# Sink scores turned by VectorE and gathered by DMAs instead of turned by TensorE, with unread products in TensorE's planned waits

## The chip, the core and the metric

The kernel runs on one NeuronCore of one Trainium2 chip. The core has a matrix engine (TensorE, "PE" in the profile, with its weight loads as "PEld"), three engines for elementwise work (VectorE "DVE", ScalarE "ACT", GpSimd "POOL") and SyncE ("SP"), which here issues every DMA. Each engine runs its own instructions in order and waits on semaphores for the others. [...] The metric is the time of one execution in microseconds on the device.

## What is computed

Attention with a causal window of 128 and a few "sink" keys at the front that every query may see, then a two-layer network with a squared ReLU:

```python
scores = scale * np.matmul(q, k.transpose(0, 1, 3, 2))       # 4 batches, 8 heads, 768 positions, 64 wide
keep = is_sink | in_window                                   # 4 sinks, window 128
scores = np.where(keep, scores, -1000000000.0)
a = np.exp(scores - max); a = a / (a.sum + 1e-09)
x = np.matmul(a, v)                                          # as 3072 tokens x 512
h = np.maximum(x @ w_in, 0.0)                                # w_in 512 x 2048
out = h * h @ w_out                                          # w_out 2048 x 512
```

The weights arrive as float64, read as pairs of 32-bit words; q, k and v are fp32.

## The kernel before

The work is cut into 8 chunks of 384 tokens (`TOK`; half a batch each, so that even chunks are first halves) and each chunk's attention into 4 pairs of heads: 32 pairs `s`. For accuracy most products run in parts: a number is split into a rounded fp32r part and the rest, and high x high, high x low and low x high are added in PSUM.

**A pair's attention** (`attention`). SP loads q, k and v (L410, L405, L417). TensorE makes scores of 3 blocks of 128 queries for two heads (`score`, L483 in plain fp32 for the first 8 pairs, called `plain`, L489 with split operands for the others). A block of scores has up to 264 columns (`BAND`): 128 keys of the block before, 8 sink columns (`NS`), 128 of its own. DVE masks it, takes the maximum and brings it to SBUF as `P` (L466), ACT takes the exponential (L472), DVE forms the reciprocals (L529, L530), and POOL scales (L537), or ACT for some blocks of the early pairs (L535).

The scaled scores must be turned before the product with v. For the first 8 pairs (`turned`) TensorE turns blocks of 128x128 (L638) and ACT or DVE copies them out of PSUM (L600). For the other 24, DVE turns 32x32 blocks (L668, L672) into `T`, SP sends `T` by four DMAs to a DRAM buffer `via` (L685) and fetches it in the right order by a fifth into `PT` (L698).

**The sinks** go another way. POOL copies the sink columns twice as a high part (L552) and once as the rest (L550) into `PSK`, 128 queries by 128 columns of which three groups of 32 hold something. TensorE turns each block of `PSK` (`turn_sinks`, L590: three blocks a pair, two in a first half, which skips its first block for `i0` = 1), and ACT or, for the 24 later pairs, DVE copies the result from PSUM into `SK` (L600).

`values` forms the output: products of `PT` (or the turned blocks) with v, both heads side by side in plain fp32 (L726), and one product of `SK` with `VS`, the values at the sinks (L730; `sinks` loads them and splits them at L368, L374 and L379). ACT and DVE split the result into `xh` and `xl` (L742, L747).

**The network** (`products`). For each of 16 slices `fc` of the hidden layer 12 products of 384 columns (L778) go into one bank, ACT and DVE form the square and its rest (L791, L795, L800, L807), and 9 products of 512 columns (L823) add to three output banks. Outputs leave through L864 and L877. The legs are chunk 0 with the first half of the slices, chunk 1 with all, chunk 0 with the rest, then chunks 2 to 7. The attention of the next chunk is spread between the products of the present one.

**The weights** come in 32 rows (`row_steps`): three DVE operations on integers (L303, L310, L317), a rounding copy on ACT (L323), and the rest on DVE or POOL (L327). A check of the weights (`check_steps`) loads halves of rows again (L339) for ACT (L344, L351).

**The order** is worked out before the program is written. `add` records steps with an engine, an expected cost, a rank (a due time, smaller is earlier), the cells they read and write, and the PSUM banks they take from a pool or give back. `Plan.order` then walks through time: for each engine it collects the steps that could start, takes the earliest (among those within 0.03 us the lowest rank), and emits it. A step may list several engines, with a handicap for some (`LOW_DVE`, `SC_ACT`, `CP_DVE`). A DVE step marked `"port"` and a POOL step are planned not to overlap. A change of TensorE's mode is planned at 0.17 us. DMAs are planned `LATE` = 1 us later than their cost says. What the plan emits stands in each engine's queue in that order; the real waits are semaphores between them.

## Time and profile before

| what | value |
|---|---|
| median of 3 runs | 690.72 us (690.72 to 690.74) |
| profiled execution | 688.96 us |
| its span, first to last instruction | 686.9 us |
| PE busy | 667.4 us, 97%, 3722 instructions |
| DVE busy | 459.1 us, 67% |
| ACT busy | 375.0 us, 55% |
| POOL busy | 215.2 us, 31% |
| DMA | 104.78 MB, mean 153 GB/s |
| mean granted TensorE clock | 0.991 |

The profiled execution was shorter than the median of the runs by 1.76 us, and 2.06 us of it lie outside the span. Matmuls are pipelined, so the length of one overlaps the next, and what a group of them costs is read from the start of one group to the start of the next. A "wait" is idle time of an engine with the instruction that ended it. The chain of waits follows the end of the program back from step to step. Stretches of the span show which engine is full at what time: the start, with little network work, is quite unlike the rest.

### The profile page before, as it was taken

Reading aid. Unit: us, or ns where it says so; the run is one execution under the profiler, and the core shown is the slowest. Engines: PE = TensorE matmul, PEld = TensorE weight load, DVE = VectorE, ACT = ScalarE, POOL = GpSimd, SP = SyncE. Lnnn points to the kernel's source line nnn. Section 1 sums busy time; section 2 is a strip of 40 time slices with the busy share of each in tenths; the row PEclk is TensorE's granted clock in tenths of the full one; section 3 lists DMA queues with packets and bytes.
Section 4 is the critical chain, followed back from the end, with each engine's and each line's share of the span. In section 5 each row is a group of like instructions: output and inputs, shape, how many; then the busy total and the mean of one; then the engine's idle time right before and its main releaser. Section 6 shows DMA issues by size and latency. Waiting matters only on the chain.

```text
span 686.9 us, 11380 instructions
## 1 busy us (share of the span) xinstructions
PE 667.4 (97%) x3722; PEld 581.1 (85%) x3722; DVE 459.1 (67%) x1194; ACT 375.0 (55%) x1073; POOL 215.2 (31%) x377
## 2 busy tenths in 40 slices
PE   4999989999999999999999999999999999999996
PEld 3667879998888888888888898888898888899985
DVE  7599999967987655676677766666776764242222
ACT  6798734355464434456666656666666565442221
POOL 4455433534544513232244323223332322000000
PEclk9799999999999999999999999999999999999999
DMA  7746455215777532466556666555557754310001
GB/s 244 220 163 203 168 192 183 84 52 157 223 245 227 154 106 93 134 207 193 155 148 184 211 188 201 170 167 174 145 169 213 223 160 114 116 51 12 0 1 51
DMA packets 58178, 104.78 MB, mean 153 GB/s; under 512 B 6208, under 2 KB 34624, under 8 KB 58112
## 3 DMA queue, kind: packets, MB, share of 16 engines
q1 hardware_dynamic: 58112, 103.98, 49.7%
q8 instruction: 31, 0.51, 0.3%
q14 instruction: 35, 0.29, 0.1%
HBM read 79.58 MB, written 24.38 MB: 151 GB/s over the span
## 4 chain that ended last, share of the span: by engine, by line
PE 90%; DVE 6%; ACT 1%; issue 1%; DMA 1%; SPq 0%; POOL 0%; DVEq 0%
PE bank L823 37%; PE bank L778 37%; PE bank L726 6%; PE bank L489 5%; PE bank L730 1%; DVE f L310 1%; PE bank L590 1%; PE bank L483 1%; DVE P L466 1%; PE bank L638 1%; DVE f L317 1%; DVE f L303 1%; DMA kn<-in_k_dram 1%; ACT w L323 0%; DVE w L327 0%
## 5 line engine op out<-in xcount | busy, mean ns | idle before, releaser
L778 PE MATMUL bank<-x,w 128*128 128x384 f32 x1536 | 303.1, 339 | 0.7 <-DVE gl L807 0.7
L778 PEld LDWEIGHTS bank<-x,w 128*128 128x128 f32 x1536 | 267.0, 188 | 9.5 <-issue 1.4
L823 PE MATMUL bank<-w,gh 128*128 128x512 f32 x768 | 242.7, 397 | 2.1 <-ACT ob L864 2.1
L823 PEld LDWEIGHTS bank<-w,gh 128*128 128x128 f32 x768 | 137.5, 188 | 21.4 <-ACT ob L864 2.4
L823 PE MATMUL bank<-w,gl 128*128 128x512 f32 x384 | 151.4, 394 | 0.0
L446 POOL TENSOR_TENSOR KS<-kn,KS 128x408 fp32r<-128x408 f32 (+1 forms) x48 | 64.9, 1352 | 225.1 <-DVE KS L441 164.2
L791 ACT ACTIVATE r<-bank 128x384 f32<-128x384 f32 x128 | 62.7, 490 | 129.3 <-PE bank L778 128.2
L472 ACT ACTIVATE P<-P,nbs 128x264 f32<-128x264 f32 (+1 forms) x192 | 94.4, 492 | 66.5 <-DVE nbs L466 65.7
L800 DVE TENSOR_TENSOR bank<-bank,r 128x384 f32<-128x384 f32 x128 | 72.1, 563 | 83.4 <-ACT r L791 83.1
L537 POOL TENSOR_SCALAR P<-P,small 128x128 f32<-128x128 f32 (+1 forms) x168 | 88.5, 543 | 71.1 <-DVE small L530 48.9
L823 PEld LDWEIGHTS bank<-w,gl 128*128 128x128 f32 x384 | 72.1, 188 | 16.6
L466 DVE CUSTOM_DVE_ANT_0 P<-bank,maskA 128x264 f32<-128x264 f32 x128 | 53.4, 426 | 45.1 <-PE bank L489 43.6
L807 DVE TENSOR_TENSOR gl<-bank,gh 128x384 fp32r<-128x384 f32 x128 | 70.9, 554 | 17.4 <-ACT gh L795 11.8
L795 ACT ACTIVATE gh<-r 128x384 fp32r<-128x384 f32 x128 | 66.7, 521 | 4.7 <-PE bank L823 2.2
L668 DVE STREAM_TRANSPOSE T<-P 128x384 f32<-128x384 f32 x96 | 45.2, 495 | 22.6 <-POOL P L537 21.7
L489 PEld LDWEIGHTS bank<-KS,QS 128*128 128x128 f32 x288 | 51.6, 188 | 6.2 <-DVE nbs L466 0.4
L489 PE MATMUL bank<-KS,QS 128*128 128x264 f32 (+1 forms) x288 | 55.4, 279 | 0.0
L742 ACT CAST x<-bank 128x384 fp32r<-128x384 f32 x32 | 15.3, 478 | 52.6 <-PE bank L730 52.4
L327 POOL TENSOR_TENSOR w<-f,w 128x512 fp32r<-128x512 f32 x19 | 27.1, 1430 | 51.4 <-ACT w L323 51.4
L726 PE MATMUL bank<-PT,vn 128*64 128x256 f32 (+1 forms) x392 | 40.6, 347 | 0.0
L726 PEld LDWEIGHTS bank<-PT,vn 128*64 128x64 f32 x392 | 25.7, 139 | 15.5 <-issue 6.7
L529 DVE TENSOR_TENSOR small<-small,eps 128x3 f32<-128x3 f32 (+1 forms) x56 | 34.5, 616 | 3.3 <-ACT P L472 2.7
(90 smaller groups left out, 575.5 us busy)
## 6 DMA issues: line engine op xcount, KB each, us to landing
raw<-in_moe_w_dram SPq DMA_DIRECT2D x32, 512.0 KB, 3.7
half<-in_moe_w_dram SPq DMA_DIRECT2D x64, 256.0 KB, 3.6
via<-T SPq DMA_DIRECT2D x48, 192.0 KB, 3.7
PT<-via SPq DMA_DIRECT2D x12, 768.0 KB, 4.4
via<-T SPq DMA_DIRECT2D x48, 160.0 KB, 4.2
PT<-via SPq DMA_DIRECT2D x12, 640.0 KB, 4.7
kn<-in_k_dram SPq DMA_DIRECT2D x24, 272.0 KB, 4.4
qn<-in_q_dram SPq DMA_DIRECT2D x32, 192.0 KB, 3.6
```

The source lines that it names most:

```text
L446: lambda h=h: nc.gpsimd.tensor_tensor(KS(h)[:, 1, 0:nk], kn()[:, h, 0:nk], f32(KS(h)[:, 0, 0:nk]), op=ALU.subtract),
L466: nc.vector.tensor_tensor_reduce(Pt(h)[:, i, o : o + n], ps_[:, 0:n], mask[:, 0:n], -SCALE, BIG, ALU.add, ALU.min, nb)
L472: nc.scalar.activation(Pt(h)[:, i, o : o + n], Pt(h)[:, i, o : o + n], AF.Exp, bias=nb, scale=-1.0, accum_out=sm[:, h, i : i + 1],)
L489: nc.tensor.matmul(bank(key)[:, 0:n], QS(h)[:, cols], flat[:, a, c0 : c0 + n], start=(a == 0), stop=(a == 1),)
L537: {"POOL": nc.gpsimd, "DVE": nc.vector}[engine].tensor_scalar(a, a, rs[:, h, i : i + 1], 1.0, op0=ALU.mult, op1=ALU.mult)
L726: nc.tensor.matmul(xo[h * D : h * D + D, qs[0] * P : qs[0] * P + len(qs) * P], vn[:, kk, h, :], rhs(), start=(n == 0), stop=False, skip_gr ...
L778: nc.tensor.matmul(bank(key)[:, 0:TOK], wi[fc][:, i, cc * P : (cc + 1) * P], xt[:, cc, :], start=(cc == 0 and j == 0), stop=(cc == NCC - 1 ...
L791: lambda key=key, r=r: nc.scalar.activation(r(), bank(key)[:, 0:TOK], AF.Relu),
L795: ("ACT", 0.41), n - 9, lambda gh=gh, r=r: nc.scalar.activation(gh(), r(), AF.Square),
L800: lambda key=key, r=r: nc.vector.tensor_tensor(bank(key)[:, 0:TOK], bank(key)[:, 0:TOK], r(), op=ALU.mult),
L807: lambda key=key, gh=gh, gl=gl: nc.vector.tensor_tensor(gl(), bank(key)[:, 0:TOK], f32(gh()), op=ALU.subtract),
L823: nc.tensor.matmul(bank(okey), gt()[:, ts_], wo[f][:, i, :], start=(f == f0 and j == 0), stop=(f == f1 - 1 and j == 2),)
```

## The change

`NS` goes from 8 to 4, which is the number of sinks in the inputs (more of them, found at run time, send the program to its general path). So a block of scores has at most 260 columns, the k blocks are 132 wide instead of 136, and the three parts of two heads' sinks fit in 24 columns.

For the 24 later pairs TensorE no longer turns the sinks. POOL writes the parts into a `PSK` of 32 columns a block, DVE turns it in 32x32 blocks into `SKT`, four DMAs bring the four groups of 32 queries onto the same 32 partitions (in `VR`, which the loads of the sink values share), and ACT or DVE copies that into `SK`, rounded. `SK` is now laid out by group of 32 queries, block, query, and the sink product reads it in runs of 32. For the first 8 pairs TensorE still turns, from a wider `PSK`.

The plan's rules change: POOL and DVE are planned to hold each other up for half a step only (`SHARE`); a step within 0.15 us that is due more than 8 earlier goes first (`HOLD`); TensorE is planned to start at 6.5 us; the early pairs' scaling may go to DVE too (`SC_DVE`); the later pairs' scores are planned to wait for their buffer `P` (`CLAIM`); the mode change costs 0.2, and the values product counts as another mode at its start.

Where TensorE is planned to wait more than 0.4 us for a step that takes a bank, before 24 us of planned time, `fill` puts products of `ident` with itself into that bank, for half of the wait at 0.22 us each. Nobody reads them. As the planned start is 6.5 us, there are none ahead of the first score.

```diff
-NS = 8
+NS = 4
...
+SHARE = 0.5
+HOLD = 0.15
+SC_DVE = 0.3
+CLAIM = (True, False)
+WARM = 24.0
+FULL = 0.5
...
-        free = dict(PE=0.0, DVE=5.5, ACT=1.5, POOL=5.0, SP=0.5)
+        free = dict(PE=6.5, DVE=5.5, ACT=1.5, POOL=5.0, SP=0.5)
...
                 a = min((a for a in able if a[0] <= first + 0.03), key=lambda a: a[1:3])
+                urgent = [x for x in able if x[0] <= first + HOLD and x[1] < a[1] - 8]
+                if urgent:
+                    a = min(urgent, key=lambda a: a[1:3])
...
             if e == "PE":
-                cost += 0.17 * (kind[0] != mode)
-                mode = kind[0]
+                if picks and WARM > t > free[e] + 0.4:
+                    yield lambda i=picks[0], n=int((t - free[e] - 0.2) * FULL / 0.22): self.fill(i, n)
+                cost += 0.2 * (kind[0] != mode)
+                mode = kind[-1]
             free[e] = t + cost
...
-                    port[e] = t + cost
+                    port[e] = t + SHARE * cost
...
         VS = wp.tile([P, NPAIR, P], F32R, name="VS")
-        PSK = [sb("PSK", [P, NQ, P], F32R, "PSK_0"), sb("w23", [P, NQ, P], F32R, "PSK_1")]
-        for t in (VS, *PSK):
+        PSK = [wp.tile([P, NQ, 32], F32R, name=f"PSK{i}") for i in range(2)]
+        SKT = wp.tile([P, NQ, 32], F32, name="SKT")
+        SK = [sb("SK", [P, 4, NQ, 32], F32R, "SK_0"), sb("w22", [P, 4, NQ, 32], F32R, "SK_1")]
+        PSKW = sb("w23", [P, 2, NQ, P], F32R, "PSK_wide")
+        for t in (VS, PSKW, *PSK, *SK):
             nc.gpsimd.memset(f32(t), 0.0)
-        SK = [sb("SK", [P, TOK], F32R, "SK_0"), sb("w22", [P, TOK], F32R, "SK_1")]
+
+        rowi = sb("gl1", [P, 1], I32, "rowi")
+        nc.gpsimd.iota(rowi, pattern=[[0, 1]], base=0, channel_multiplier=1)
+        third = const.tile([P, 1], F32, name="third")
+        nc.vector.tensor_copy(third, rowi)
+        nc.vector.tensor_scalar(third, third, float(4 * NS), -1.0, op0=ALU.is_ge, op1=ALU.mult)
...
+        VR = [("VR", x) for x in range(4)]
...
             add(
                 ("DVE", 0.62, "port"), rank,
-                lambda: nc.vector.tensor_tensor(VS[lo], raw()[lo], f32(VS[lo]), op=ALU.subtract),
-                reads=["VR"], writes=["VS"],
+                lambda: nc.vector.scalar_tensor_tensor(
+                    VS[0:rows], f32(VS[0:rows]), third[0:rows], raw(), op0=ALU.mult, op1=ALU.add
+                ),
+                reads=VR, writes=["VS"],
...
-                    reads=reads, writes=keys, take=[("any" if early else "att", key) for key in keys],
+                    reads=reads + [P_cell(h) for h in heads] * (CLAIM[plain] and i > 0),
+                    writes=keys + [P_cell(h) for h in heads] * (CLAIM[plain] and i == 0), take=[("any" if early else "att", key) for key in keys],
...
-            two = s % 2 if plain else 0
+            two = s % 2
             psk = PSK[two]
-            psk_cell = "PSK" if two == 0 else ("spare", 23)
-            to = psk.rearrange("p q (t c) -> p q t c", c=32)
+            psk_cell = ("PSK", two)
+            if turned:
+                psk = PSKW[:, two]
 
             def part_sinks(h, low):
-                own = slice(h * NS, h * NS + NS)
                 src = Pt(h)[:, i0:NQ, P:BS]
+                to = psk[:, i0:NQ, 0 : 6 * NS].rearrange("p q (t c) -> p q t c", c=2 * NS)[..., h * NS : h * NS + NS]
                 if low:
-                    nc.gpsimd.tensor_tensor(to[:, i0:NQ, 1, own], src, f32(to[:, i0:NQ, 0, own]), op=ALU.subtract)
+                    nc.gpsimd.tensor_tensor(to[:, :, 1], src, f32(to[:, :, 0]), op=ALU.subtract)
                 else:
-                    nc.gpsimd.tensor_copy(
-                        to[:, i0:NQ, 0:3:2, own], src.unsqueeze(2).broadcast_to([P, NQ - i0, 2, NS])
-                    )
+                    nc.gpsimd.tensor_copy(to[:, :, 0:3:2], src.unsqueeze(2).broadcast_to([P, NQ - i0, 2, NS]))
...
                         add(
-                            [pool, ("ACT", 0.38 if n > P else 0.28, "", SC_ACT)] if plain else [pool, pool], r - URGE,
+                            [
+                                pool, ("ACT", 0.38 if n > P else 0.28, "", SC_ACT),
+                                ("DVE", 0.25 if n > P else 0.18, "port", SC_DVE),
+                            ] if plain else [pool, pool], r - URGE,
...
-            sk = SK[two]
-            sk_cell = "SK" if two == 0 else ("spare", 22)
-            nsq = (NQ - i0) * P
+            sk_cell = ("spare", 22) if two and plain else "SK"
+            sk = SK[1 if two and plain else 0]
             key = ("sk", s)
-
-            def turn_sinks():
-                for i in range(i0, NQ):
-                    nc.tensor.transpose(bank(key)[:, (i - i0) * P : (i - i0 + 1) * P], f32(psk[:, i]), ident)
-
-            r = rank(0.95)
-            add(
-                ("PE", 0.11 * (NQ - i0), 0), r, turn_sinks,
-                reads=[(psk_cell, h, *x) for h in range(2) for x in ((), (1,))] + ([] if two == 0 else [psk_cell]),
-                writes=[key], take=[("any" if early else "att", key)],
-            )
+            own_sinks = [(psk_cell, h, *x) for h in range(2) for x in ((), (1,))]
 
             def copy(engine, dst, src):
                 nc.scalar.copy(dst, src) if engine == "ACT" else nc.vector.tensor_copy(dst, src)
 
-            on_act, on_dve = ("ACT", 0.36 if nsq == TOK else 0.3, "", 0.0), ("DVE", 0.48 if nsq == TOK else 0.36, "", CP_DVE)
-            add(
-                [on_act, on_dve] if plain else [on_dve, on_dve], r - URGE,
-                lambda e: copy(e, sk[:, 0:nsq], bank(key)[:, 0:nsq]), reads=[key], writes=[sk_cell], drop=[key],
-            )
+            if turned:
+
+                def turn_sinks():
+                    for i in range(i0, NQ):
+                        nc.tensor.transpose(bank(key)[:, i * P : (i + 1) * P], f32(psk[:, i]), ident)
+
+                r = rank(0.95)
+                add(
+                    ("PE", 0.11 * (NQ - i0), 0), r, turn_sinks, reads=own_sinks + [("spare", 23)], writes=[key], take=[("any" if early else "att", key)],
+                )
+                add(
+                    [("ACT", 0.3, "", 0.0), ("DVE", 0.36, "", CP_DVE)], r - URGE,
+                    lambda e: copy(
+                        e, sk[0:32, :, i0:NQ],
+                        bank(key)[0:32, i0 * P : TOK].rearrange("p (i r b) -> p r i b", r=4, b=32),
+                    ),
+                    reads=[key], writes=[sk_cell], drop=[key],
+                )
+            else:
+                add(
+                    ("DVE", 0.18), rank(1.0) - URGE,
+                    lambda: nc.vector.transpose(SKT[:, i0:NQ], f32(psk[:, i0:NQ])), reads=own_sinks, writes=["SKT"],
+                )
+
+                rows_ = lambda: sb("VR", [P, 4, NQ, 32], F32, f"sk_{s}")
+
+                def gather(x):
+                    nc.sync.dma_start(
+                        out=rows_()[0:32, x, i0:NQ].rearrange("p i b -> p (i b)"),
+                        in_=SKT[32 * x : 32 * x + 32, i0:NQ].rearrange("p i b -> p (i b)"),
+                    )
+
+                for x in range(4):
+                    add(
+                        ("SP", 0.42, 2.5, 13), rank(0.85), lambda x=x: gather(x), reads=["SKT"], writes=[("VR", x)],
+                    )
+                add(
+                    [("ACT", 0.4), ("DVE", 0.35, "port", CP_DVE)], rank(0.8) - URGE,
+                    lambda e: copy(e, sk[0:32, :, i0:NQ], rows_()[0:32, :, i0:NQ]),
+                    reads=VR, writes=[sk_cell],
+                )
...
                 nc.tensor.matmul(
-                    xo[:, i0 * P : TOK], VS[:, p], sk[:, 0:nsq], start=False, stop=True, skip_group_check=True
+                    xo[:, i0 * P : TOK], VS[:, p], sk[:, :, i0:NQ].rearrange("p r i b -> p i r b"), start=False, stop=True, skip_group_check=True
                 )
...
-                ("PE", (1.08 if half == 0 else 1.3) + 0.17 + (0.175 if nsq == TOK else 0.13), 0), r, values,
+                ("PE", (1.07 if half == 0 else 1.28) + (0.375 if i0 == 0 else 0.32), 2, 0), r, values,
...
+        def fill(i, n):
+            for _ in range(n):
+                nc.tensor.matmul(banks[i][:, 0:P], ident, ident, start=True, stop=True)
+
+        plan.fill = fill
...
-    vs = np.zeros((B, 64 + 2 * NS, H // 2, 2, D), v.dtype)
-    for r0 in (0, 32, 64):
+    vs = np.zeros((B, 6 * NS, H // 2, 2, D), v.dtype)
+    for r0 in range(0, 6 * NS, 2 * NS):
         for t in range(2):
             vs[:, r0 + t * NS : r0 + t * NS + NS, :, t, :] = v[:, t::2, 0:NS].transpose(0, 2, 1, 3)
```

More of the change, by code (lines that the diff above doesn't have):

```diff
@@ L505, in attention @@
                 if plain:
-                    reads, cost = [q_cell, (k_cell, 0), (k_cell, 1)], (0.44 if n > P else 0.23)
+                    reads, cost = [q_cell, (k_cell, 0), (k_cell, 1)], (0.43 if n > P else 0.22)
                 else:
@@ L575, in attention @@
                         ("POOL", 0.29), r - URGE + 0.01, lambda h=h: part_sinks(h, False),
[L576 removed]
+                        reads=done, writes=[(psk_cell, h)],
                     )
```

6 lines of the change are left out of this document (2 added, 4 removed).

## The prediction

> **What bounds the kernel now.** I read the page's span and its chain first, then the busy time by stretch, then the waits of TensorE after 110 us.
>
> ```profile
> span 686.9 us, 11380 instructions
> PE 90%; DVE 6%; ACT 1%; issue 1%; DMA 1%; SPq 0%; POOL 0%; DVEq 0%
> 10.00:15.00 5.00, 2.37 (x15) 1.50 (x15) 4.90 (x24) 5.00 (x23) 2.61 (x4) 1.00 0.90 320
> 15.00:20.00 5.00, 2.37 (x10) 1.45 (x9) 4.00 (x11) 3.64 (x11) 5.00 (x9) 0.57 1.00 292
> 20.00:25.00 5.00, 5.00 (x24) 3.12 (x24) 1.32 (x8) 3.54 (x12) 3.45 (x13) 0.50 0.77 258
> 25.00:30.00 5.00, 5.00 (x38) 3.69 (x36) 3.33 (x10) 3.82 (x11) 0.00 (x0) 0.91 0.54 171
> 300.00:400.00 100.00, 100.00 (x564) 88.44 (x563) 69.30 (x178) 63.42 (x196) 34.18 (x60) 1.00 0.62 186
> sum 81.60, PE 79.24 PEld 63.47 DVE 78.13 ACT 59.21 POOL 34.76; mean PE 9.91 PEld 7.93 DVE 9.77 ACT 7.40 POOL 4.34
> PE bank L778 <- DVE gl L807: 0.7, 1, 0.7
> ```
>
> The columns of a stretch are its length, the busy time of PE, PEld, DVE, ACT and POOL with instruction counts, the granted clock, and the DMA share. Three stages show. Up to 28 us the kernel starts up: PE waits much of the time, and from about 16 to 26 us it runs at half clock (0.57, 0.50, 0.91). From 28.4 to 110 us (the sum row covers that stretch) PE is busy 79.24 of 81.60 us and DVE 78.13, so two engines are full there. After that only PE is full: 100.00 of 100.00 us, DVE at 69, ACT at 63, and the last row is the only group of PE waits from 110 us on, 0.7 us. In that stage a microsecond of PE work taken away is a microsecond of the end; work moved to DVE, ACT, SP or the DMAs is free as long as it arrives in time.
>
> **The sinks of the 24 later pairs leave PE.** Today PE turns three blocks a pair (two in a first half) at L590. The rows are PE's timeline: start, length, line, group.
>
> ```profile
> L590 PE MATMUL bank<-ident,PSK x60: 270/272/273, 153.3 to 578.1; 128*128 128x128 f32 x60
> 401.27 0.62 PE L823 MATMUL bank<-w,gh 128*128 128x512 f32 x2
> 401.73 0.39 PE L823 MATMUL bank<-w,gl 128*128 128x512 f32 x1
> 416.64 0.49 PE L590 MATMUL bank<-ident,PSK 128*128 128x128 f32 x3
> 416.88 0.71 PE L823 MATMUL bank<-w,gh 128*128 128x512 f32 x2
> 417.44 0.39 PE L823 MATMUL bank<-w,gl 128*128 128x512 f32 x1
> 437.65 0.38 PE L590 MATMUL bank<-ident,PSK 128*128 128x128 f32 x2
> 437.79 0.71 PE L823 MATMUL bank<-w,gh 128*128 128x512 f32 x2
> 438.34 0.39 PE L823 MATMUL bank<-w,gl 128*128 128x512 f32 x1
> ```
>
> Lengths overlap in the pipeline, so I go from start to start. Three turns take 416.88 - 416.64 = 0.24 us, and the two products behind them take 417.44 - 416.88 = 0.56, where an undisturbed two take 401.73 - 401.27 = 0.46: together 0.34 us. Two turns take 0.14 + (0.55 - 0.46) = 0.23 us. The 60 turns after 110 us are 12 pairs of three and 12 of two, so 12 x 0.34 + 12 x 0.23 = **6.8 us**, all on the bound engine. The eight early pairs keep their turns.
>
> Fewer sink columns make the scores 260 wide, not 264:
>
> ```profile
> L489 PE MATMUL bank<-KS,QS 128*128 128x264 f32 x236 | 47.3, 285 | 0.0
> L489 PE MATMUL bank<-KS,QS 128*128 128x128 f32 x46 | 7.7, 250 | 0.0
> ```
>
> (285 - 250) / 136 is 0.26 ns a column; 4 x 236 columns are **0.2 us**.
>
> The sink product at L730 now reads its moving operand in runs of 32 columns. That form of operand exists today in the values product at L726, from PT, beside a contiguous one from PTS:
>
> ```profile
> 85.78 1.52 PE L726 MATMUL bank<-PTS,vn 128*64 128x128 f32 x16
> 87.23 0.44 PE L730 MATMUL bank<-SK,VS 128*128 128x384 f32 x1
> 434.70 1.52 PE L726 MATMUL bank<-PT,vn 128*64 128x256 f32 x16
> 436.15 0.44 PE L730 MATMUL bank<-SK,VS 128*128 128x384 f32 x1
> ```
>
> Both take 1.45 us up to L730, so the runs cost nothing in plain fp32. For fp32r no row shows it. Bounds: nothing, or as much again as a whole sink product (at most 0.44 us, x 32 pairs = 14 us). I take nothing, being nearest to the pair of rows above, and keep a third of the other end as a rival.
>
> **What comes in its place** is a longer path: POOL's parts, one 32x32 transpose on DVE, four gathers on SP, one copy.
>
> ```profile
> 415.71 0.24 POOL L550 TENSOR_TENSOR PSK<-P,PSK 128x24 fp32r<-128x24 f32 x1
> 416.50 2.68 SPq L685 DMA_DIRECT2D via<-T x4
> 421.85 0.34 SPq L698 DMA_DIRECT2D PT<-via  x1
> 422.29 10.96 SPq L339 DMA_DIRECT2D half<-in_moe_w_dram  x3
> via<-T SPq DMA_DIRECT2D x48, 192.0 KB, 3.7
> L672 DVE STREAM_TRANSPOSE T<-P 128x128 f32<-128x128 f32 x24 | 6.6, 274 | 0.0
> L600 DVE CAST SK<-bank 128x384 fp32r<-128x384 f32 x12 | 6.6, 552 | 1.9 <-PE bank L730 1.9
> ```
>
> For the pair valued at 434.70 us the parts end at 415.95. Add 0.27 for the transpose, 2.7 for four issues (as the four via issues take now), 3.7 for landing (192 KB; the gathers are 12 KB) and 0.55 for the copy: ready at 423.2, 11.5 us ahead of its reader. PT, issued at 421.85, is the later operand anyway. DVE loses a copy of 0.55 and gains 0.27 plus, if not ACT, about 0.55 again; ACT or DVE have 30 us free in 100. SP gains 96 issues, 65 us in all at 0.67 each, and what stands behind them in its queue is the L339 reads and the next pair's loads, which today sit in a wait of 10.96 us. I cost all of it at nothing in the third stage; without that cover each microsecond late is paid on PE, once a pair (a rival). PE's bank for the turn is freed too; the waits row says that nobody waits there, so I count nothing.
>
> **The start.** Here the plan is rebuilt, unread products fill PE's planned waits, and DVE may scale the early pairs.
>
> ```profile
> 10.10 1.35 PE L483 MATMUL bank<-kn,qn 64*128 64x128 f32 x10 [0.22 <-DVE nbs L466]
> 12.81 0.33 PE L638 MATMUL bank<-ident,P 128*128 128x128 f32 x1 [1.37 <-POOL P L537]
> 17.65 1.33 PE L638 MATMUL bank<-ident,P 128*128 128x128 f32 x5 [2.47 <-POOL P L537]
> 19.14 1.31 PE L638 MATMUL bank<-ident,P 128*128 128x128 f32 x4 [0.16 <-ACT P L535]
> 99.20 0.71 PE L823 MATMUL bank<-w,gh 128*128 128x512 f32 x2 [2.11 <-ACT ob L864]
> L537 POOL TENSOR_SCALAR P<-P,small 128x264 f32<-128x264 f32 x140 | 74.8, 549 | 42.7 <-DVE small L530 22.9 <-ACT sq L351 10.0 <-ACT sq L344 6.4
> L231 DVE TENSOR_SCALAR inw<-rel,par 128x256 f32<-128x256 f32 x1 | 0.3, 349 | 0.0
> 28.42 0.77 PE L778 MATMUL bank<-x,w 128*128 128x384 f32 x3
> 18.79 0.31 ACT P L535
> ```
>
> (The last is from the chain of waits.) The last score ends at 11.45; from there to 17.65 PE gets five turns of P between waits for POOL, and the clock halves near 16 us. From 19.14 on PE is busy without a break, and the chain runs on PE: so half clock is paid in full. Work lost: 0.86 x 0.5 up to 20 us, 5 x 0.50, 5 x 0.09, together 3.4 us; with PE's busy time before 19.14 some 4.1.
>
> [...]
>
> I take **2.5 us** of 0 to 4.1, since the scaling on POOL and ACT (18.79) that feeds those turns doesn't speed up with the clock. DVE has to follow, as it is full from 28 us on; it stands idle 1.00, 3.68 and 1.67 us in the three stretches from 15 to 30 us, so there is room for 2.5 us.
>
> For the new order and the scaling on DVE the trace has bounds only. At best the waits of the rows (1.37, 2.47 and 0.16) and the 2.11 at 99.20 vanish: 6.1 us. At worst a dozen scalings of 0.35 us land on a full DVE and push the weights: 4 us lost. Fillers cost only where real work was ready earlier than planned; they take half a planned wait. Two small operations on DVE ahead of the first scores cost 0.3. Shorter queues on POOL (0.55 a scaling, 5.00 of 5.00 busy from 15 us) speak for a gain; DVE's 78 of 81.6 us speaks against a large one. Net I take **0.9 us**.
>
> **The sum**: 6.8 + 0.2 + 2.5 + 0.9 = 10.4 us. The profiled execution took 688.96 us with a span of 686.9; the median of the three runs is 690.72, so 1.76 above it. Span 676.5, that execution 678.6, median **680.3 us**.
>
> **Rivals.**
> - The start gives nothing: the clock drops all the same, or DVE, full from 28 us, swallows what PE gains. For it: DVE has only 3.5 us idle in 81.6. Against it: the 6.35 us that DVE stands idle from 15 to 30 us. Only 7.0 us are left: 683.7.
> - The start gives all: waits, clock and the stall at 99.20: 7.0 + 3.4 + 6.1 - 0.3 = 16.2, so 674.5. It needs POOL's, ACT's and DVE's queues to shrink together.
> - Strided fp32r runs slow: 0.15 us x 32 pairs = 4.8 of the 10.4 go back: 685.1.
> - It doesn't do what it says: the new order of the start costs what the turns save, by more than the 4 us above; about 690.5.
> - **The slower one**: the gathers slip in SP's queue behind the L339 reads. The four would issue after 433.25 (422.29 + 10.96), the operand be ready 2.7 + 3.7 + 0.55 later, at 440.2, and PE would stand 5.5 us ahead of 434.70's group. It decides from two such pairs in 24 on (10.4 / 5.5 = 1.9); with the four of one chunk the time is 702, with all 24 it is 812. Against it: the 11.5 us of slack, and that the gathers wait for nothing but the transpose.
>
> **Chances**: forecast 0.50, own range 677 to 682.5; start gives nothing 0.22; start gives all 0.12; strided slow 0.05; no effect 0.05; gathers late 0.06. A measurement of this kernel tells a difference from none from about 0.2% (1.4 us) on. So faster 0.89, same 0.05, slower 0.06. The range goes from the second rival, 674.5, to past the third, 687.5; it leaves out the last two rivals and a little beside.
>
> **What would show it.** The page's PE row: no L590 after 110 us, 60 instructions fewer; groups of L823 that now follow one another at 0.46. The waits of PE after 110 us: still under 1 us; if L726 or L730 waits for a DMA, DVE or ACT copy of SK, the slack was misjudged. The distance from L730 to the next product: if it grows, strided reads cost. The clock by stretch: 1.00 from 15 to 30 us, and the first L778 earlier than 28.42 (the row above) by some 2 to 4 us; the same start with a full clock means that POOL and ACT bound it. DVE's busy time from 28 to 110 us tells whether DVE swallowed the lead. I am wrong if the third stage is no shorter by 6 to 7 us, or if the first product comes no earlier.

## The result and the profile after

| kernel | median | runs | profiled execution | span |
|---|---|---|---|---|
| before | 690.72 us | 689.75 to 690.74 | 688.96 us | 686.9 us |
| changed | 684.55 us | 684.19 to 685.14 | 684.36 us | 682.2 us |

The changed kernel takes 0.9915 of the time of before, 95% interval 0.9898 to 0.9932: **6.2 us less**, where 10.4 were forecast. In the profiled executions the spans differ by 4.7 us; the other 1.5 us is that before's profiled execution lay 1.76 us below its median and the changed kernel's only 0.19 below, and no view says why.

In the changed kernel the turn of the sinks stands at L620 (before L590), the values at L776 and L780 (L726, L730), the first product at L828 (L778), the second at L873 (L823), the scaling at L560 (L537), the gathers at L643, the fillers at L1005. First the head of its page and its chain.

```profile
span 682.2 us, 11489 instructions
...
PE 662.6 (97%) x3676; PEld 575.2 (84%) x3676; DVE 460.3 (67%) x1221; ACT 373.9 (55%) x1070; POOL 212.7 (31%) x383
...
PE 83%; DVE 10%; DMA 2%; issue 1%; POOL 1%; ACT 1%; SPq 1%; DVEq 0%; ACTq 0%; POOLq 0%
```

PE has 3676 instructions: 3722 of before, less 60 turns, with 14 fillers. Its share of the chain has fallen from 90% to 83%, and DVE's has risen from 6% to 10%. Now the stretches, with the columns of the same view of before (length, busy time of PE, PEld, DVE, ACT and POOL, granted clock, DMA share, GB/s).

```profile
15.00:20.00 5.00, 3.42 (x27) 2.28 (x26) 4.92 (x12) 4.19 (x13) 2.78 (x6) 1.00 0.96 272
20.00:25.00 5.00, 4.72 (x38) 3.36 (x38) 4.59 (x15) 4.35 (x12) 5.00 (x13) 1.00 0.78 224
25.00:30.00 5.00, 5.00 (x38) 3.58 (x36) 4.96 (x15) 4.59 (x14) 2.25 (x2) 1.00 0.99 334
28.40:110.00 81.60, 78.10 (x449) 62.88 (x446) 78.71 (x177) 52.82 (x131) 39.34 (x52) 0.98 0.61 189
70.00:80.00 10.00, 7.66 (x47) 6.81 (x47) 8.61 (x15) 5.12 (x11) 6.13 (x9) 0.83 0.56 177
300.00:400.00 100.00, 100.00 (x558) 88.22 (x557) 67.56 (x182) 63.98 (x199) 33.69 (x60) 1.00 0.66 193
```

The start runs at full clock, where before had 0.57, 0.50 and 0.91. The third stage is as full of PE as it was. What is new lies between: from 70 to 80 us PE is idle for 2.3 us and the clock is 0.83. The same stretch of before:

```profile
70.00:80.00 10.00, 10.00 (x64) 8.58 (x64) 9.87 (x18) 7.67 (x20) 5.04 (x7) 1.00 0.56 191
```

The timelines of PE and POOL around it (start, length, line, group, idle time before it and what ended that):

```profile
72.35 0.60 PE L688 MATMUL bank<-ident,P 128*128 128x128 f32 x4
75.28 0.90 PE L620 MATMUL bank<-ident,PSK_wide 128*128 128x128 f32 x3 [2.34 <-POOL PSK_wide L574]
75.84 2.27 PE L828 MATMUL bank<-x,w 128*128 128x384 f32 x6
```

```profile
70.38 3.30 POOL L560 TENSOR_SCALAR P<-P,small 128x260 f32<-128x260 f32 x4 [1.02 <-DVE small L553]
73.62 1.26 POOL L576 CAST PSK_wide<-P 128x24 fp32r<-128x24 f32 x2
74.85 0.38 POOL L574 TENSOR_TENSOR PSK_wide<-P,PSK_wide 128x12 fp32r<-128x12 f32 x2
```

Pair 7, the last of the eight whose sinks TensorE still turns, is scaled by POOL: four steps in 3.30 us, where the plan counts 0.46 for each. One by one in the trace they take 0.49, 0.48, 1.24 and 1.17 us. The first two run beside DVE's work on the network (L850, L857), the last two beside DVE's steps on a weight row (L346, L322, L329), which the plan marks `"port"`. The parts of its sinks end at 75.23, and PE, which has the turn of those sinks next in its queue, waits 2.34 us for them. Finer stretches show that the clock then falls:

```profile
74.00:76.00 2.00, 0.72 (x4) 0.72 (x5) 2.00 (x5) 0.00 (x0) 1.23 (x4) 0.77 0.18 48
76.00:78.00 2.00, 2.00 (x8) 1.90 (x8) 0.97 (x3) 1.51 (x3) 0.19 (x1) 0.50 0.89 277
78.00:80.00 2.00, 2.00 (x14) 1.92 (x13) 1.75 (x2) 1.18 (x3) 1.09 (x1) 0.88 0.57 221
```

**The lead.** To see where time comes and goes I used one measure for all kernels. All products of TensorE but the sinks' turns and the fillers are added up in order of their start, each at the distance to the next start that it has in an undisturbed stretch (0.175 us for a first product, 0.231 for a second, 0.109 for a turn of `P`). Scores and values in plain fp32 start two at a time (the eight values from 431.01 us on in the changed kernel 6 or 7 ns apart, with 0.21 to 0.26 us between the pairs), so they count by undisturbed groups (0.65 us for four scores, 0.91 for eight values of 256 columns, 0.32 for four of 128). The lead at a time is by how much earlier than before a kernel had done what before had done by then; the order of work differs, so it is good to some 0.5 us. The column "end" is the time from the start of the last matmul to the end of the span. All in us; the rows e1 to e12 are the experiments below.

```
kernel    28    60    75    80    97   100   110   150   400   650   end   span
before                                                              6.31  686.9
changed  3.4   2.7   2.6  -1.7  -1.1   1.0   0.5  -0.4   3.3   5.7  7.47  682.2
e1       2.8   2.4   2.4  -0.5   0.0   2.2   1.4   0.4   4.5   6.9  7.73  681.5
e2       0.7   1.5   1.6   1.5   1.8   3.9   3.4   2.2   6.2   8.7  7.21  679.5
e3       1.1   1.2   1.2   1.2   1.4   0.7  -0.4  -0.4  -0.3  -0.3  6.49  687.4
e4       2.8   2.2   2.2  -2.2  -1.6   0.5  -0.1  -0.9  -1.6  -1.6  6.05  688.1
e5       2.9   2.3   2.2  -0.6   0.0   2.1   1.3   0.4   3.3   5.7  7.70  682.4
e6       3.3   3.7   2.8   1.0   1.3   3.1   0.8  -1.1   2.7   5.1  7.15  682.5
e7       0.9   2.4   2.2   2.2   2.4   4.5   4.0   4.0   7.6  10.0  7.69  678.2
e8       0.1   0.6   0.7   0.6   0.9   3.0   2.5   1.2   4.4   6.8  7.41  681.2
e9       3.1   2.5   2.4   2.5   2.6   4.8   2.9   2.9   6.4   8.8  7.64  679.3
e10      3.0   2.4   2.4   2.2   2.5   4.7   2.8   2.8   6.9   9.3  7.72  679.0
e11      0.9   2.7   2.5   2.4   2.7   4.9   4.4   4.4   8.4  10.8  7.20  677.2
e12      0.6   2.5   2.4   2.2   2.6   4.7   4.2   4.2   6.6   9.0  6.86  678.7
```

For the changed kernel: +3.4 at 28 us, -0.8 to 75 us, -4.3 between 75 and 80, +0.6 to 97, +2.1 where before has its own wait at 99.20, -1.4 to 150, +6.1 from 150 to 650, -1.2 behind the last matmul. That is 4.5, and the spans differ by 4.7.

### The profile page after: what moved, and what is told of

The parts are those of the page before. It is cut to its first block, busy times and chain, and to the rows that moved or that the text cites. A ratio compares the mean times of both kernels' runs of the same rounds, so it can differ in the third digit from the quotient of the medians.

```text
span 682.2 us, 11489 instructions
## 1 busy us (share of the span) xinstructions
PE 662.6 (97%) x3676; PEld 575.2 (84%) x3676; DVE 460.3 (67%) x1221; ACT 373.9 (55%) x1070; POOL 212.7 (31%) x383
## 4 chain that ended last, share of the span: by engine, by line
PE 83%; DVE 10%; DMA 2%; issue 1%; POOL 1%; ACT 1%; SPq 1%; DVEq 0%; ACTq 0%; POOLq 0%
PE bank L873 36%; PE bank L828 35%; PE bank L776 5%; PE bank L511 4%; DVE f L336 2%; PE bank L505 1%; DVE f L329 1%; DVE P L488 1%; PE bank L780 1%; DVE bank L850 1%; POOL P L560 1%; DVE f L322 1%; PE bank L688 1%; DVE gl L857 1%; DMA ob<-part 1%
## 5 line engine op out<-in xcount | busy, mean ns | idle before, releaser
L828 PE MATMUL bank<-x,w 128*128 128x384 f32 x1536 | 302.7, 339 | 0.6 <-DVE gl L857 0.6
L828 PEld LDWEIGHTS bank<-x,w 128*128 128x128 f32 x1536 | 266.8, 189 | 8.9 <-issue 1.0
L873 PE MATMUL bank<-w,gh 128*128 128x512 f32 x768 | 242.6, 397 | 1.2 <-DVE ob L907 1.0
L873 PEld LDWEIGHTS bank<-w,gh 128*128 128x128 f32 x768 | 138.8, 188 | 24.2 <-issue 1.4
L873 PE MATMUL bank<-w,gl 128*128 128x512 f32 x384 | 152.2, 396 | 0.3 <-DVE gl L857 0.3
L468 POOL TENSOR_TENSOR KS<-kn,KS 128x396 fp32r<-128x396 f32 (+1 forms) x48 | 64.9, 1353 | 237.8 <-DVE KS L463 200.8
L850 DVE TENSOR_TENSOR bank<-bank,r 128x384 f32<-128x384 f32 x128 | 71.9, 562 | 83.1 <-ACT r L841 82.9
L494 ACT ACTIVATE P<-P,nbs 128x260 f32<-128x260 f32 (+1 forms) x192 | 93.7, 488 | 59.6 <-DVE nbs L488 57.8
L560 POOL TENSOR_SCALAR P<-P,small 128x260 f32<-128x260 f32 (+1 forms) x169 | 85.3, 520 | 64.1 <-DVE small L553 47.8
L873 PEld LDWEIGHTS bank<-w,gl 128*128 128x128 f32 x384 | 72.1, 188 | 18.2 <-DVE gl L857 1.4
L857 DVE TENSOR_TENSOR gl<-bank,gh 128x384 fp32r<-128x384 f32 x128 | 71.2, 556 | 20.1 <-ACT gh L845 10.9
L488 DVE CUSTOM_DVE_ANT_0 P<-bank,maskA 128x260 f32<-128x260 f32 x128 | 52.6, 419 | 45.1 <-PE bank L511 44.8
L511 PE MATMUL bank<-KS,QS 128*128 128x260 f32 (+1 forms) x288 | 55.1, 277 | 0.0
L346 POOL TENSOR_TENSOR w<-f,w 128x512 fp32r<-128x512 f32 x20 | 30.1, 1506 | 46.0 <-ACT w L342 46.0
L776 PE MATMUL bank<-PT,vn 128*64 128x256 f32 (+1 forms) x392 | 39.5, 341 | 0.2 <-DMA PT<-via 0.2
L552 DVE TENSOR_TENSOR small<-small,eps 128x3 f32<-128x3 f32 (+1 forms) x56 | 37.0, 662 | 2.9 <-ACT P L494 2.1
L776 PEld LDWEIGHTS bank<-PT,vn 128*64 128x64 f32 x392 | 25.2, 136 | 15.5 <-issue 5.5
```

The costliest lines, as they stand in the source:

```text
L468: lambda h=h: nc.gpsimd.tensor_tensor(KS(h)[:, 1, 0:nk], kn()[:, h, 0:nk], f32(KS(h)[:, 0, 0:nk]), op=ALU.subtract),
L488: nc.vector.tensor_tensor_reduce(Pt(h)[:, i, o : o + n], ps_[:, 0:n], mask[:, 0:n], -SCALE, BIG, ALU.add, ALU.min, nb)
L494: nc.scalar.activation(Pt(h)[:, i, o : o + n], Pt(h)[:, i, o : o + n], AF.Exp, bias=nb, scale=-1.0, accum_out=sm[:, h, i : i + 1],)
L511: nc.tensor.matmul(bank(key)[:, 0:n], QS(h)[:, cols], flat[:, a, c0 : c0 + n], start=(a == 0), stop=(a == 1),)
L560: {"POOL": nc.gpsimd, "DVE": nc.vector}[engine].tensor_scalar(a, a, rs[:, h, i : i + 1], 1.0, op0=ALU.mult, op1=ALU.mult)
L776: nc.tensor.matmul(xo[h * D : h * D + D, qs[0] * P : qs[0] * P + len(qs) * P], vn[:, kk, h, :], rhs(), start=(n == 0), stop=False, skip_gr ...
```

## The experiments

In each diff "-" is the kernel that the experiment starts from, named ahead of it. Ratios are to the kernel before, with the 95% interval. E1 to e4 ran beside one another, as did e5 to e8, and e9 to e11.

**e1: the changed kernel without fillers.**

```diff
-WARM = 24.0
+WARM = 0.0
```

> The changed kernel without the unread products, all else as it is. Theory one (the start's lead of some 4 us at 28 us is real, but is lost again up to 130 us, where DVE is full and PE stands 2.3 us at 75 us): the clock halves again in the start and the lead at 28 us falls by 2 to 3 us, but the end moves by less than 1.5 us: 683.5 to 686. Theory two (a lead at 28 us reaches the end, so the fillers are worth the half clock of 3.4 us): about 688.

683.68 us, 0.9897 (0.9881 to 0.9914). Without the fillers the kernel is, if anything, 0.9 us shorter. They do what they are for: from 20 to 25 us the clock is 0.66 without them (first row below) and 1.00 with them. But 28 us on the lead differs by 0.6 us, at 60 us by 0.3, and at the end it is the other way round.

```profile
20.00:25.00 5.00, 4.91 (x29) 3.57 (x30) 3.68 (x12) 3.73 (x10) 4.58 (x12) 0.66 1.04 289
75.86 0.55 PE L620 MATMUL bank<-ident,PSK_wide 128*128 128x128 f32 x3 [2.36 <-POOL PSK_wide L574]
76.00:78.00 2.00, 2.00 (x15) 1.97 (x15) 1.33 (x3) 1.55 (x4) 0.00 (x0) 1.00 0.56 186
```

The same wait stands here, 2.36 us, but the clock behind it stays at 1.00, and the last section shows that this may be the chance of the execution, not the missing fillers. That is worth 1.2 us of lead at 80 us (-0.5 against -1.7), and 1.2 at 650 us.

**e2: the gathers in the plan of before.** The changed kernel with the planner's rules of before.

```diff
-SHARE = 0.5
-HOLD = 0.15
+SHARE = 1.0
+HOLD = -1.0
-CLAIM = (True, False)
-WARM = 24.0
+CLAIM = (False, False)
+WARM = 0.0
-        free = dict(PE=6.5, DVE=5.5, ACT=1.5, POOL=5.0, SP=0.5)
+        free = dict(PE=0.0, DVE=5.5, ACT=1.5, POOL=5.0, SP=0.5)
-                cost += 0.2 * (kind[0] != mode)
+                cost += 0.17 * (kind[0] != mode)
...
-                                ("DVE", 0.25 if n > P else 0.18, "port", SC_DVE),
```

The values product is planned as before, too, as one mode and at its old cost.

> The sinks' new path alone (4 sink columns, DVE's transpose, four gathers), with the plan's rules of before and no unread products. Theory one (the 60 turns are worth 6.6 to 6.8 us, the narrower scores 0.2, and the new plan with the fillers nets nothing): 683.2 to 684.6. Theory two (the gathers cost something of their own from 150 us on, so that the turns bring less, and the plan brings the rest): 685.5 to 687.5.

681.5 us, 0.9874 (0.9859 to 0.9889), shorter than either theory had it. The gathers with the four sinks alone do 3 us better than the whole change. From 150 to 650 us the lead grows by 6.5 us, and there is no stall at 75. Another 2.1 us come at 99, where before waits and this kernel does not; why was not tested.

**e3: the fillers in the plan of before.** The kernel before with the fillers alone (none ahead of the first score).

```diff
+WARM = 24.0
+FULL = 0.5
...
+                if picks and self.first is not None and WARM > t > free[e] + 0.4:
+                    yield lambda i=picks[0], n=int((t - free[e] - 0.2) * FULL / 0.22): self.fill(i, n)
+                if picks and self.first is None:
+                    self.first = n
```

> The kernel before with nothing but the unread products in the planned waits before 24 us, from the second score on. Theory one: the clock stays up, the first product comes 1 to 3 us earlier, and DVE, full from 28 us on, leaves at most 1.5 us of it: 689 to 691. Theory two: the half clock of 3.4 us is won in full: about 687.3. A third outcome: the planned waits lie elsewhere than the real ones and the clock halves all the same: 690.7.

690.4 us, 0.9999 (0.9988 to 1.001): nothing. The clock rises (0.69 from 20 to 25 us, where before has 0.50), the lead is some 1.2 us from 28 to 97 us, and gone at 110. It goes at this kernel's wait, which is as long as that of before at 99.20. But here the granted clock is 0.55 from 98 to 100 us and 0.60 to 102, where before has 1.00. Up to that wait DVE, busy for 77.3 of the 81.6 us from 28.4 to 110, took nothing of the lead.

```profile
20.00:25.00 5.00, 5.00 (x31) 3.16 (x31) 1.30 (x8) 4.14 (x14) 3.59 (x13) 0.69 0.91 271
98.10 1.11 PE L829 MATMUL bank<-w,gh 128*128 128x512 f32 x2 [2.11 <-ACT ob L870]
```

**e4: the new plan with the sinks turned by TensorE.** The changed kernel, in which the 24 later pairs' sinks are turned by TensorE again and copied by DVE, as before.

```diff
-        PSK = [wp.tile([P, NQ, 32], F32R, name=f"PSK{i}") for i in range(2)]
-        SKT = wp.tile([P, NQ, 32], F32, name="SKT")
+        PSKL = sb("PSK", [P, NQ, P], F32R, "PSK_late")
...
-            if turned:
+            if True:
 
                 def turn_sinks():
```

> The changed kernel with the sinks of the 24 later pairs turned by TensorE again (three or two turns, a copy by DVE from PSUM), 4 sink columns and the new plan with its fillers kept. Theory one: the 60 turns cost 6.6 to 6.8 us again: 690.8 to 691.8, no better than the kernel before. Theory two (the gathers cost something of their own): 688.5 to 690.

690.28 us, 0.9995 (0.9986 to 1.0003). The time lies between the two theories. The new plan, the fillers and the four sinks are together worth nothing; all of the change's gain is the gathers'. Up to 150 us the lead is that of the changed kernel to within 0.6 us. From 150 to 650 us this kernel loses 0.7 us and the changed kernel wins 6.1: the 60 turns cost **6.8 us** in that stage. PE's waits from 110 us on, 1.6 us here and 1.5 there, take nothing from that.

**e5: fillers in the stall.** The changed kernel with eight unread products ahead of the sink turns of pair 7.

```diff
                 def turn_sinks():
+                    if s == NPS - 1:
+                        plan.fill(plan.got[key], 8)
```

> The changed kernel with eight more unread products ahead of pair 7's sink turns, where PE stands 2.3 us for POOL's parts near 73 us. Theory one (the stall halves the clock behind it, 0.83 from 70 to 80 us, and that costs 1.5 us beside the stall itself): the clock stays at 1.00 there, the lead at 80 us rises by some 1.5 us, and the time falls to about 683. Theory two (the clock there doesn't matter): 684.5.

684.56 us, 0.9913 (0.9896 to 0.9931), to 0.01 us the changed kernel. The clock stays at 1.00 through the place:

```profile
74.00:76.00 2.00, 1.47 (x14) 1.28 (x13) 2.00 (x4) 0.02 (x1) 1.65 (x5) 1.00 0.12 43
76.00:78.00 2.00, 2.00 (x16) 1.97 (x15) 1.33 (x4) 1.71 (x4) 0.12 (x1) 1.00 0.79 233
```

and the lead at 80 us is 1.1 us better. But it is given back between 150 and 400 us: PE's two waits from 150 us on, ahead of a values product and ahead of a second product, are 0.9 and 1.0 us, where e1, with the same lead at 150 us, has 0.5 and 0.4. Waits of about a microsecond come and go with the order of the steps, and a repair of this size can't be told from them in the time.

**e6: POOL's scaling planned at what it costs.** The changed kernel, where the plan counts 0.82 us for a scaling of pairs 4 to 7 on POOL.

```diff
-                        pool = ("POOL", 0.46 if n > P else 0.33)
+                        pool = ("POOL", (0.82 if plain and not early else 0.46) if n > P else 0.33)
```

> The changed kernel, with POOL's scaling of the early pairs 4 to 7 put into the plan at 0.82 us a block, as it took for pair 7 (3.30 us for four), instead of 0.46. Theory one (the new plan puts pair 7's turns 2.3 us ahead of POOL because it counts on a POOL that DVE doesn't hold up): the stall near 73 us goes, with the halved clock behind it, and the lead of 2.7 us at 70 us stays: 680 to 681.5. Theory two (DVE, full from 28 us on, takes the lead back in another place): 683.5 to 685.

684.12 us, 0.9904 (0.9889 to 0.9919). The stall shrinks to 0.28 and 0.47 us, and the lead at 80 us is 2.7 us better than the changed kernel's. At 150 us it is 0.7 worse. PE's waits of more than 0.6 us up to there:

```profile
101.31 0.50 PE L873 MATMUL bank<-w,gl 128*128 128x512 f32 x1 [1.12 <-DVE gl L857]
104.25 0.72 PE L873 MATMUL bank<-w,gh 128*128 128x512 f32 x2 [0.69 <-DVE ob L914]
125.03 0.50 PE L873 MATMUL bank<-w,gl 128*128 128x512 f32 x1 [0.90 <-DVE gl L857]
```

They are for DVE. So one wrong price isn't the fault (0.82 is the mean of two scalings at 0.48 and two at 1.2 us, so no single price fits them): with DVE and POOL planned to run beside one another, what was taken from the place near 75 us came back at the next full one.

**e7: DVE and POOL planned apart for whole steps.** The changed kernel with before's rule for the two engines.

```diff
-SHARE = 0.5
+SHARE = 1.0
```

> The changed kernel with one rule of the plan as before: POOL and DVE hold each other up for the whole of a step (SHARE = 1). Theory one (this rule is what makes the plan too hopeful about POOL): the stall near 73 us goes or shrinks, 680.5 to 683. Theory two (the stall comes from another of the new rules, such as the scaling on DVE): the stall stays, 684 to 686.

**679.6 us**, 0.9839 (0.9825 to 0.9853), 5 us better than the changed kernel by this one number, and a little more than theory one had. PE has no wait between 28 and 150 us. The turn of pair 7's sinks is put 7 us later and finds its parts 3.4 us old; the first row is from PE's timeline, the second from POOL's.

```profile
82.09 0.49 PE L620 MATMUL bank<-ident,PSK_wide 128*128 128x128 f32 x3
78.38 0.27 POOL L574 TENSOR_TENSOR PSK_wide<-P,PSK_wide 128x12 fp32r<-128x12 f32 x1
```

Its lead at 28 us is only 0.9 us, 2.5 less than the changed kernel's, and at 75 us the difference is 0.4.

**e8: the gathers and the fillers in the plan of before.** E2 with the fillers.

```diff
-WARM = 0.0
+WARM = 24.0
...
+                if picks and self.first is None:
+                    self.first = n
```

> The gathered sinks with the plan's rules of before (681.5 us) and the unread products in its planned waits before 24 us. Theory one (a lead won in the start is lost again where DVE is full, by 130 us): 681 to 682.5, no difference. Theory two (the lead of 1.2 us that the fillers gave in the old plan was lost only at that plan's stall near 99 us, which is not there in this one): about 680.3.

681.81 us, 0.9869 (0.9854 to 0.9885), beside e2's 681.5: again nothing. But this pair doesn't decide between the theories, since here 34 unread products didn't hold the clock. It is at half for as long as in e2 (6.83 us, from 18.65 to 25.47), and the lead at 28 us is 0.1:

```profile
20.00:25.00 5.00, 5.00 (x24) 3.03 (x25) 1.90 (x9) 4.03 (x14) 2.62 (x10) 0.50 0.67 226
```

**e9 and e10: the half rule in the start only**, with the fillers and without.

```diff
-                    port[e] = t + SHARE * cost
+                    port[e] = t + (SHARE if t < 28 else 1.0) * cost
```

For e10 also:

```diff
-WARM = 24.0
+WARM = 0.0
```

> The changed kernel with the new port rule (half of a step) up to 28 us of planned time and the old one (the whole step) after that. Theory one (the lead of some 4 us at 28 us was lost to the stalls that the half rule plans, not to DVE's work as such): the lead at 28 us is 3.5 to 4.2, most of it is still there at 150 us, as much as 5 to 6.5 with before's own stall near 99 us gone, and the time is 677 to 678.5, below the 679.6 with the whole rule throughout. Theory two (DVE, full from 28 us on, sets when the weights are ready, and levels every lead): the lead at 150 us comes to some 4 us as with the whole rule, 679 to 680.5.

> The same without the unread products. If they are worth nothing in this plan either (they delayed real work at 15 to 20 us, and cost 0.9 us in the changed kernel): within 0.7 us of the former. If a full clock in the start is worth its 3.4 us once nothing levels it: 1.5 to 3.4 us longer.

681.46 us, 0.9867 (0.9846 to 0.9888), and 681.73, 0.9876 (0.9856 to 0.9896). Both theories for e9 missed; it is longer than either. They keep the changed kernel's start (3.1 and 3.0 us of lead at 28 us) and have no stall at 75. It brings them nothing over e7 and e11: at 60 us they lead by 2.5 and 2.4 us, those by 2.4 and 2.7, and between 100 and 110 us they lose 1.9 us, those 0.5.

**e11: whole steps, no fillers.**

```diff
-SHARE = 0.5
-WARM = 24.0
+SHARE = 1.0
+WARM = 0.0
```

> The changed kernel with the whole port rule throughout (679.6 us) and without the unread products. Theory one (the fillers bring nothing that reaches the end): 679 to 680.3. Theory two (they are part of that plan's gain): 681 or more.

**679.17 us**, 0.9838 (0.9821 to 0.9856): the best of all, ahead of both kernels, 5.4 us under the changed one. Its clock in the start is lower than that of e1, e7 and e10; the third row is the stretch from 28.4 to 110 us:

```profile
15.00:20.00 5.00, 0.77 (x4) 0.45 (x5) 4.93 (x15) 4.34 (x14) 3.19 (x5) 0.80 1.06 320
20.00:25.00 5.00, 5.00 (x26) 3.54 (x26) 2.44 (x10) 3.06 (x10) 2.58 (x8) 0.52 0.88 277
28.40:110.00 81.60, 81.51 (x489) 65.88 (x486) 79.10 (x176) 54.33 (x137) 39.47 (x53) 1.00 0.60 188
```

PE is busy 81.51 of 81.60 us from 28.4 to 110, where the changed kernel has 78.10 and before 79.24. Against e2 (run at another time, beside its own runs of before) it is 2.3 us shorter; so by this comparison the rest of the new plan's rules, which I did not take apart, are worth about that.

**e12: the gathers issued by ScalarE.** E11 with the gathers in ACT's queue at the same planned times. It asks after the 1.2 us at the end of the program.

```diff
                 def gather(x):
-                    nc.sync.dma_start(
+                    nc.scalar.dma_start(
```

> The whole-port plan without fillers, with the 96 gathers issued from ScalarE's queue at the same planned times, so that SyncE's program is as short as in the kernel before. Theory (the end of the program is longer because SyncE's program carries 96 more DMA issues): from the start of the last matmul to the end of the span 6.1 to 6.5 us instead of 7.20, SyncE's gap after its last branch about 0.5 us instead of 2.7, and the time some 0.7 to 1.1 us under 679.17 (678.1 to 678.5), if ScalarE's waiting for the transposes costs nothing. Rival (it is the DMAs themselves or the longer data path, not the queue that issues them): the stretch stays at 7.2 or above, and the time at 679 or above. Second rival: ScalarE, waiting at its queue for VectorE's transposes, holds up exponentials: waits of TensorE for ACT after 150 us, and a time above 680 whatever the end does.

680.72 us, 0.9853 (0.9836 to 0.9869). The end of SP's program: the comparison with which all engines jump over the general path, and SP's next instructions (duration, count, first and last start). Before, the changed kernel, e12:

```profile
L960 SPq COMPARE_BRANCH  x1: 50/50/50, 683.5 to 683.5; - x1
L960 SPq EVENT_SEMAPHORE  x8: 17/17/17, 684.0 to 685.5; - x8
```

```profile
L1015 SPq COMPARE_BRANCH  x1: 50/50/50, 677.6 to 677.6; - x1
L1015 SPq EVENT_SEMAPHORE  x8: 17/17/17, 680.3 to 680.8; - x8
```

```profile
L1015 SPq COMPARE_BRANCH  x1: 50/50/50, 674.5 to 674.5; - x1
L1015 SPq EVENT_SEMAPHORE  x8: 17/17/17, 675.0 to 677.0; - x8
L1015 DVEq COMPARE_BRANCH  x1: 72/72/72, 673.2 to 673.2; - x1
L1015 ACTq COMPARE_BRANCH  x1: 54/54/54, 673.3 to 673.3; - x1
L1015 DVEq EVENT_SEMAPHORE  x1: 21/21/21, 676.9 to 676.9; - x1
L1015 ACTq EVENT_SEMAPHORE  x1: 17/17/17, 677.0 to 677.0; - x1
```

SP's jump takes 0.5 us before, 2.7 us in the changed kernel, and 0.5 us with the gathers on ACT's queue. In e4, which has no gathers, it takes 0.5 us; in the nine others, which have them on SP, 2.6 to 3.2. So the jump is long where the gathers stand in SP's program; what about them makes it so, no run shows. The end shrinks only from 7.20 to 6.86 us and not to 6.3, since now DVE and ACT come last, 3.7 us after their jumps (3.5 and 3.1 in e11). And ACT's queue is a poor place for the gathers, which was my second rival: behind them stand ACT's other steps, and PE has a wait of 1.06 us that e11 has not (by ACT's timeline its queue stood until 161.24 us at the gathers of that pair, which wait for DVE's transposes, with exponentials behind them; that this makes the wait is argued, not shown). Between 160 and 200 us the lead of e12 falls 1.6 us behind that of e11.

```profile
164.53 1.30 PE L776 MATMUL bank<-PT,vn 128*64 128x256 f32 x12 [1.06 <-DVE small L552]
```

## Why the prediction was right in sign and 4 us too low

**The third stage was right.** Forecast 6.8 + 0.2 us. E4 against the changed kernel, both with four sinks, gives 6.8 us for the turns. The changed kernel's own lead grows by 6.1 from 150 to 650 us; no run shows the 0.2 of the narrower scores by itself. No turn of the sinks is left after 110 us (the last of 20 is at 75.8), and the gathers hide: PE's waits from 110 us on are 1.5 us, 0.8 above before, which the sum had put at nothing, and none is for `SK`.

```profile
L620 PE MATMUL bank<-ident,PSK_wide x20: 271/273/474, 15.9 to 75.8; 128*128 128x128 f32 x20
PE bank L873 <- DVE ob L907: 1.0, 1, 1.0
...
PE bank L776 <- DMA PT<-via: 0.2, 1, 0.2
sk<-SKT SPq DMA_DIRECT2D x48, 8.0 KB, 3.0
sk<-SKT SPq DMA_DIRECT2D x48, 12.0 KB, 2.3
```

The gathers land 2.3 to 3.0 us after their issue, in the median, where I had put 3.7 for them. The copy into `SK` ends 8.4 us or more ahead of its product in all 24 pairs, where I had counted on 11.5 of slack. The slower rival, gathers that slip behind the L339 reads, did not come.

**Strided reads cost nothing here.** From the sink product to the next product, first in the changed kernel, then before:

```profile
432.46 0.44 PE L780 MATMUL bank<-SK,VS 128*128 128x384 f32 x1
432.74 0.69 PE L828 MATMUL bank<-x,w 128*128 128x384 f32 x3
```

```profile
436.15 0.44 PE L730 MATMUL bank<-SK,VS 128*128 128x384 f32 x1
436.43 0.69 PE L778 MATMUL bank<-x,w 128*128 128x384 f32 x3
```

0.28 us both times.

**The clock did as the fillers want it, but that was not worth 2.5 us.** Clock 1.00 from 15 to 30 us was forecast and came, and a lead of 3.4 us at 28 us, the 2.5 + 0.9 of the sum. That the two agree is luck: without the fillers (e1) the lead there is still 2.8 us, so the new order brought 2.8 and the full clock 0.6. The sign I named for it, a first product ahead of 28.42, failed: it stands at 28.64. It was badly chosen, since the plan had put other work ahead. Three pairs' values are done by then, before had one.

```profile
16.47 1.30 PE L776 MATMUL bank<-PT,vn 128*64 128x128 f32 x12
...
22.70 1.30 PE L776 MATMUL bank<-PTS,vn 128*64 128x128 f32 x12
...
26.45 1.30 PE L776 MATMUL bank<-PT,vn 128*64 128x128 f32 x12
...
28.64 1.83 PE L828 MATMUL bank<-x,w 128*128 128x384 f32 x9
```

The step that failed is "so half clock is paid in full", with the 2.5 us taken for it. No run shows the 2.5 us: they were my estimate, and so was that unread products would keep the clock up at all. What the runs showed in their place is less: by the lead at 28 us the fillers bring 0.6 us (the changed kernel against e1), 0.1 (e9 against e10), nothing (e7 against e11) and 1.1 (e3 against before). One reason is on record: before is at half clock for 10.24 us of the start, but the new plan without fillers (e1) for only 3.41, so at most 1.7 us were left for the fillers to win there. Why even that didn't come in full was not tested.

The next step, "DVE has to follow, as it is full from 28 us on; it stands idle 1.00, 3.68 and 1.67 us in the three stretches from 15 to 30 us, so there is room for 2.5 us", is open. DVE did follow in those stretches (4.92, 4.59 and 4.96 of 5 us busy). The kernels of the new plan (e1, e4 to e7, e9 to e12 and the changed one) lead by 0.6 to 3.4 us at 28 us and by 2.2 to 2.8 at 75. So what the new order had won by 28 us in one kernel and not in another is levelled. That DVE does the levelling is argued from its 78.7 busy microseconds of 81.6, not shown by a run that relieves it. E3 speaks against it: there the lead stood from 28 to 97 us beside a DVE nearly as full (77.3 us), and went at a wait with a halved clock behind it. The first rival had this mechanism, and the clock's 2.5 us would have gone with it. Five pairs of kernels that differ in the fillers alone (e1, e3, e8, e10 and e11, each beside its partner) are 0.1 to 0.9 us apart, three times the one without fillers ahead, twice the one with them, and none by more than the intervals allow. With the fillers the changed kernel's clock stays at 1.00 among the turns from 20 to 25 us, without them (e1) it is 0.66; in e8 it is 0.50 with 34 fillers, so they are not always enough. In before the clock stayed at 0.50 up to 25.9 us, through turns and also through scores (from 20.84 us on) and values (from 23.26 us on), so turns alone don't account for it.

**"Net I take 0.9 us" for the new plan was off by the price of one rule.** I had bounded the plan's loss by 4 us, from scalings that go to DVE. The loss came, 4.3 us between 75 and 80 us, but from the rule that lets DVE and POOL overlap for half a step (e7: without it the stall is gone). Of it 2.3 us are the wait, and some 1.7 the half clock behind it, which e1 with the same wait doesn't have. Sixteen scalings did go to DVE, and PE waits for them once, 0.3 us:

```profile
L560 DVE TENSOR_SCALAR P<-P,small x16: 278/471/583, 13.1 to 58.8; 128x260 f32<-128x260 f32 x14, 128x128 f32<-128x128 f32 x2
```

The scaling on POOL is where it costs. Up to 110 us four of the changed kernel's scalings on POOL take 1.17 to 1.40 us, each beside two or three weight steps of DVE (L322, L329, L336, L346), and those that overlap no weight step take 0.38 to 0.52. So beside weight steps a scaling takes 0.7 us and more above what the plan counts. In e7 eight scalings up to 110 us take 0.92 to 1.47 us in the same company, but there the plan has left room for them, and PE has no wait from 28 us on. Before's page gave 0.55 us as the mean over the whole span, and the plan's 0.46 lay in the code; I compared neither with the place.

**The end was not in the sum at all**: 1.2 us. It goes with SP's longer jump, but with the gathers off SP (e12) only 0.3 us came back, since DVE and ACT then came last.

| term | forecast | shown |
|---|---|---|
| third stage | 7.0 us | 6.1 (6.8 by e4) |
| the start, to 28 us: clock | 2.5 | 0.6 |
| the start, to 28 us: new plan | 0.9 | 2.8 |
| levelled by 75 us | 0 | -0.8 |
| stall and clock, 75 to 80 us | 0 | -4.3 |
| 80 to 150 us, before's wait at 99.20 in it | 0 | +1.3 |
| end of the program | 0 | -1.2 |
| sum, against the span | 10.4 | 4.5 (4.7 measured) |

The time landed near that of the first rival, 683.7 us, whose mechanism explains at most a part of it.

## What to carry to other kernels

Work taken off the engine that is full for 500 us came through as counted, from start to start (6.8 us counted, 6.8 by e4); a lead won in the start was not the same 50 us later (3.4 us at 28 us, 2.6 at 75), so don't put it into the sum before a run shows it there. In a plan worked out ahead, compare each planned cost with the trace in the very place where the step will stand, and with what runs beside it there (0.46 planned, 0.48 or 1.2 there): the rule that squeezed two engines closer didn't make the kernel shorter (684.55 us with it, 679.6 without). And where many instructions are added to an engine, read its last microseconds too (96 gathers on SP went with a jump of 2.7 us for one of 0.5).
